# Attention by blocks of 128 query rows with the exponentials stationary, ahead of an ELU feed-forward layer, on one core

## The chip, the cores and the metric

One Trainium2 chip, one of its cores. The metric is the device time of one execution in microseconds; lower is better.

## What is computed

q, k and v are [8, 8, 576, 64] (batch, heads, sequence, head size). Each head attends with a bias that falls with the distance, within a window of 128 keys up to and including the query; the result, as 4608 tokens of 512 features, goes through two matrices with an ELU between them. Tokens are rows of batch and sequence, features are heads and head size.

```python
scores = q @ k^T / 8                       # [8, 8, 576, 576]
bias   = slope[h] * -|i - j|
scores = where((i - j >= 0) & (i - j < 128), scores + bias, -1e9)
attn   = softmax(scores)
x      = (attn @ v) as [4608, 512]
h      = x @ w_in                          # w_in [512, 2048]
g      = where(h > 0, h, exp(min(h, 0)) - 1)
out    = g @ w_out                         # w_out [2048, 512]
```

## The kernel before

All products run in f16 with f32 sums. The order of instructions on every engine is written out by hand: a list of steps, each with one round of the feed-forward layer (`hidden`, the `elu` of the round before, `output` of the block before) and, between them, the attention tasks put at that step with `at`. Engines run their own instructions in that order.

**Attention.** `load_qk` brings q and k of a batch by POOL's DMA queue with a cast to f16 (`stq`; the last 64 rows come by `load_tail`). `transposes` turns two heads on TensorE into one bank (`tp`), and VectorE copies the bank in two halves to `QK` (heads by q or k by position). Rows 64 to 127 of `QK` hold bias rows (`bias_rows`), so that the score product adds the distance bias and pushes far keys down. `scores` fills one bank (`sp`) with half of a head's windowed scores, transposed: keys are partitions, queries are columns. ScalarE takes the exponential to `E`, and `cut` on VectorE takes the minimum with `band`, which sets what is outside of the window to 0. `values` (and `values_tail` for the last 64 queries, `values_half` for batch 0) multiplies with V as the stationary operand and up to 256 exponentials as the moving one: V has 64 columns of ones beside it (`VP`), so that 64 rows of the result `av` are the value sums and the other 64 are the sum of exponentials. ScalarE makes the inverse of these as exp(-ln(s)) (`log_den`, `inv_den`), and VectorE multiplies into `xT` (`normalize`), which is features by tokens, as the hidden layer wants it. V comes by SP's queue in f32 (`load_v`, four transfers a block of 128 keys) and is cast by POOL (`cast_v`).

**Feed-forward.** `blocks` are 512 tokens each, the first one split into two of 256. `hidden` makes one bank of 128 features by 512 (or 256) tokens in four matmuls (`hp`, two banks in turn); ScalarE takes the exponential to `e`, POOL clips it to at most 1, and `elu` on VectorE takes max(e - 1, h) to `g`. `output` makes four matmuls a step (two for the narrow blocks) of the block that is 16 steps behind; after 16 of them ScalarE copies the one bank `op` to `ob`, and SP's queue writes it out. Hidden work begins at step 13, output at step 29; a batch of attention takes 16 steps.

Of the kernel before, what the change touches and what calls it, by code (L numbers as in the profile page):

```python
# [19 lines left out]
def kernel(  # L20
# [24 lines left out]
    ps_t = ctx.enter_context(tc.tile_pool(name="ps_t", bufs=1, space=PSUM))  # L45
# [3 lines left out]
    ident = const.tile([128, 128], F16, name="ident")  # L49
    band = const.tile([128, 1024], F16, name="band")  # L50
# [4 lines left out]

    QK = const.tile([128, H, 2, 768], F16, name="QK")

    VP = [const.tile([128, 5, NP, 256], F16, name=f"VP{g}", tag=f"VP{g}") for g in range(2)]
    w_in_sb = const.tile([128, 4, FF], F16, name="wi")
    w_out_sb = const.tile([128, NFC, DM], F16, name="wo")  # L60

    xT = const.tile([128, 4, RING], F16, name="xT")


    stq, stt, vf = {}, {}, {}

    def load_qk(b, w, hs=None):

        if b not in stq:
            stq[b] = stage.tile([128, 2, H, 4, D], F16, name="stq")  # L70
        h0, h1 = hs or (0, H)
# [10 lines left out]
    def load_v(b, n, behind=False):  # L82

        t = vf[b, n] = stage.tile([128, H, D], F32, name="vf", tag="vf", bufs=3)
        if behind:
            nc.gpsimd.memset(t[:, 0, 0:1], 0.0)
        if n < 4:
            for j in range(4):
                nc.sync.dma_start(
                    t[32 * j:32 * j + 32, :, :],  # L90
                    v[b, :, 128 * n + j:128 * n + 128:4, :].rearrange("h p d -> p h d"))
        else:
            nc.sync.dma_start(t[0:64, :, :], v[b, :, 512:576, :].rearrange("h p d -> p h d"))

    def cast_v(b, n):
        p = 128 if n < 4 else 64
        nc.gpsimd.tensor_scalar(  # L97
            out=VP[b % 2][0:p, n, :, :].rearrange("p a (g c) -> p (a g) c", g=2)[:, :, 0:64],
            in0=vf.pop((b, n))[0:p, :, :], scalar1=1.0, scalar2=0.0, op0=ALU.mult, op1=ALU.add)
# [12 lines left out]
    with tc.manual_schedule():  # L112

        row = const.tile([128, 1], I32, name="row")
        col = const.tile([128, 128], I32, name="col")
        posi = const.tile([128, 768], I32, name="posi")
        load_qk(0, 1, (0, 2))
        load_qk(0, 0, (0, 2))
        nc.gpsimd.iota(row, pattern=[[0, 1]], base=0, channel_multiplier=1)
        nc.gpsimd.iota(col, pattern=[[1, 128]], base=0, channel_multiplier=0)  # L120
        nc.gpsimd.iota(posi[:, 0:512].rearrange("p (n j i) -> p n j i", j=4, i=32),
                       pattern=[[128, 4], [1, 4], [4, 32]], base=0, channel_multiplier=0)
        nc.gpsimd.iota(posi[:, 512:768].rearrange("p (a b i) -> p a b i", b=2, i=64),
                       pattern=[[0, 2], [0, 2], [1, 64]], base=512, channel_multiplier=0)
# [12 lines left out]
        def small(name, n=1):
            return const.tile([128, n], F32, name=name, tag=name)
# [6 lines left out]
        kdiv, kmod, koff = (const.tile([128, 1], I32, name=n, tag=n) for n in ("kdiv", "kmod", "koff"))  # L145
        V.tensor_scalar(out=kdiv, in0=row, scalar1=5, scalar2=None, op0=ALU.logical_shift_right)
        V.tensor_scalar(out=kmod, in0=row, scalar1=31, scalar2=None, op0=ALU.bitwise_and)
        kmid = small("kmid")
        V.tensor_scalar(out=kmid, in0=kmod, scalar1=4.0, scalar2=63.5, op0=ALU.mult, op1=ALU.add)
        V.tensor_tensor(out=kmid, in0=kmid, in1=kdiv, op=ALU.add)  # L150
        rmid = small("rmid")
        V.tensor_scalar(out=rmid, in0=rowf, scalar1=63.5, scalar2=None, op0=ALU.add)

        bt = const.tile([128, 384], F32, name="bt")
        V.tensor_scalar(out=bt[:, 0:256], in0=posi[:, 0:256], scalar1=kmid, scalar2=None,
                        op0=ALU.subtract)
        V.tensor_tensor(out=bt[:, 0:256], in0=bt[:, 0:256], in1=bt[:, 0:256], op=ALU.mult)
        V.tensor_scalar(out=band[:, 0:256], in0=bt[:, 0:256], scalar1=4060.0, scalar2=BIG,
                        op0=ALU.is_le, op1=ALU.mult)
        V.tensor_copy(band[:, 256:512], band[:, 0:256])  # L160
# [3 lines left out]
        TQ = const.tile([128, 768], F16, name="TQ")  # L164
        TK = const.tile([128, 768], F16, name="TK")
        gt = const.tile([128, 768], F32, name="gt")
        g_, r_ = slice(64, 96), slice(96, 128)
        gi = const.tile([128, 768], I32, name="gi")
        V.tensor_scalar(out=gi[g_, :], in0=posi[g_, :], scalar1=gof[g_, :], scalar2=None, op0=ALU.add)
        V.tensor_scalar(out=gi[g_, :], in0=gi[g_, :], scalar1=255, scalar2=None, op0=ALU.bitwise_and)  # L170
        V.tensor_scalar(out=TQ[g_, :], in0=gi[g_, :], scalar1=134.5, scalar2=-30000.0,
                        op0=ALU.is_gt, op1=ALU.mult)
        V.tensor_scalar(out=TK[g_, :], in0=gi[g_, :], scalar1=7.5, scalar2=None, op0=ALU.is_lt)
# [4 lines left out]
        V.tensor_scalar(out=gt[r_, :], in0=posi[r_, :], scalar1=float(-MID), scalar2=None, op0=ALU.add)  # L178
        V.tensor_scalar(out=TK[r_, :], in0=gt[r_, :], scalar1=is96[r_, :], scalar2=is97[r_, :],
                        op0=ALU.mult, op1=ALU.add)  # L180
        V.tensor_scalar(out=TQ[r_, :], in0=gt[r_, :], scalar1=isx[r_, :], scalar2=is96[r_, :],  # L181
                        op0=ALU.mult, op1=ALU.add)
        for t0 in (576, 704):
            V.memset(TK[64:128, t0:t0 + 64], 0.0)
            V.memset(QK[0:64, :, 1, t0:t0 + 64], 0.0)

        def bias_rows(h):
            c = 8.0 * 2.0 ** (-8.0 * (h + 1) / H)
            nc.scalar.copy(QK[64:128, h, 0, :], TQ[64:128, :])  # L189
            V.tensor_copy(QK[g_, h, 1, :], TK[g_, :])  # L190
            V.tensor_scalar(out=QK[r_, h, 1, :], in0=TK[r_, :], scalar1=c, scalar2=None, op0=ALU.mult)  # L191

        def more_band():
            V.tensor_copy(band[:, 512:768], band[:, 0:256])
            V.tensor_copy(band[:, 768:896], band[:, 0:128])

            V.tensor_scalar(out=bt[:, 256:320], in0=posi[:, 512:576], scalar1=-384.0, scalar2=kmid,
                            op0=ALU.add, op1=ALU.subtract)
            V.tensor_scalar(out=bt[:, 320:384], in0=posi[:, 512:576], scalar1=-512.0, scalar2=rmid,
                            op0=ALU.add, op1=ALU.subtract)  # L200
            V.tensor_tensor(out=bt[:, 256:384], in0=bt[:, 256:384], in1=bt[:, 256:384], op=ALU.mult)
            V.tensor_scalar(out=band[:, 896:1024], in0=bt[:, 256:384], scalar1=4060.0, scalar2=BIG,
                            op0=ALU.is_le, op1=ALU.mult)

        def ones_v(g):
            nc.gpsimd.memset(VP[g][:, :, :, 64:128], 1.0)
            nc.gpsimd.memset(VP[g][64:128, 4, :, :], 0.0)


        ex, avt, tailt, lden, rden = {}, {}, {}, {}, {}  # L210
        HI, LO = slice(64, 128), slice(0, 64)
        NUM, DEN = (LO, HI), (HI, LO)

        def transposes(b, hp):
            t = ps_s.tile([128, 2, 2, 4, 2, 32], F16, name="tp", tag="sps")
# [7 lines left out]
            for odd in range(2):  # L223
                r = slice(64 * odd, 64 * odd + 64)
                V.tensor_copy(  # L225
                    QK[0:64, 2 * hp:2 * hp + 2, :, 0:512].rearrange(
                        "p h w (n a i) -> p (h w) n a i", a=2, i=32)[:, :, :, odd, :],
                    t[r, :, :, :, :, :].rearrange("p h w n a i -> p (h w) (n a) i"))

        def transposes_tail(b):  # L230
# [7 lines left out]
            c0 = 512 + 128 * (b % 2)  # L238
            for g in range(2):
                r = slice(64 * g, 64 * g + 64)  # L240
                V.tensor_copy(
                    QK[0:64, :, :, c0:c0 + 64].rearrange("p (n g) w c -> p n g w c", g=2)[:, :, g, :, :],
                    t[r, :, :, :])

        def scores(b, hp, g, half):

            if b == 0 and half == 0:
                s = ps_h.tile([128, 512], F32, name="sp0", tag="hp")
            else:
                s = ps_s.tile([128, 512], F32, name="sp", tag="sps")  # L250
            kq = QK[:, 2 * hp + g, :, :]
            c0 = 512 + 128 * (b % 2)
            if half == 0:
                mm = [(0, 0, 0, 256), (128, 256, 128, 256)]
            else:
                mm = [(256, 0, 256, 256), (384, 256, 384, 128), (384, 384, c0, 64), (c0, 448, c0, 64)]
            for kc, o, qc, n in mm:
                nc.tensor.matmul(s[:, o:o + n], kq[:, 1, kc:kc + 128], kq[:, 0, qc:qc + n],  # L258
                                 start=True, stop=True)
            if half == 0:  # L260
                ex[b, hp, g] = work.tile([128, 1024], F16, name="E", tag="E", bufs=9)
# [282 lines left out]
```

## Time and profile before

| | us |
|---|---|
| median of 3 runs (lowest to highest) | 396.51 (396.01 to 397.08) |
| the profiled execution | 397.05 |
| its span, from the first to the last instruction | 395.3 |

| engine | busy, us | share of the span | instructions |
|---|---|---|---|
| TensorE, matmuls (PE) | 342.1 | 87% | 2440 |
| TensorE, weight loads (PEld) | 202.6 | 51% | 2440 |
| VectorE (DVE) | 262.9 | 67% | 448 |
| ScalarE (ACT) | 246.1 | 62% | 465 |
| GpSimd (POOL) | 158.8 | 40% | 261 |

Busy time of TensorE counts each matmul from its start to its modelled end; matmuls overlap, so the busy share says where it had work, and not how close to its peak it ran. Weight loads overlap matmuls. An engine named with a q (POOLq, SPq) is the part of it that issues transfers. L361 is line 361 of the kernel.

### The profile page before, as it was taken

The numbers are of one execution on the slowest core, as the hardware profiler recorded it, in microseconds if no ns is written. First come the engines' busy times: TensorE is split into PE (matmuls) and PEld (weight loads), VectorE is DVE, ScalarE is ACT, GpSimd is POOL, SyncE is SP. The second block draws the span as 40 slices with busy tenths as digits, with TensorE's granted clock in tenths as the row PEclk, the third lists the DMA queues.
The fourth block names the chain that finished last, engine by engine and source line by source line (L and its number), as shares of the span: only waits on it lengthen the run. The fifth ranks groups of instructions, "written<-read, shape, count | busy, mean of one in ns | idle before, by whom it ended". The sixth has DMA issues, their size and how long they took to land.

```text
span 395.3 us, 6838 instructions
## 1 busy us (share of the span) xinstructions
PE 342.1 (87%) x2440; PEld 202.6 (51%) x2440; DVE 262.9 (67%) x448; ACT 246.1 (62%) x465; POOL 158.8 (40%) x261
## 2 busy tenths in 40 slices
PE   1234775998999899999999999999999999999984
PEld 0112553675565455567765555555666544444431
DVE  6776677688788877777776778777876533343300
ACT  1445565788777866877687778776777643443411
POOL 8692173264365246334623452433222333333300
PEclk9999998799999999999999999999999999999999
DMA  6999999149339138632933293311111112121122
GB/s 85 158 163 188 192 172 149 24 62 157 80 39 169 39 89 106 104 77 64 146 82 82 46 142 80 90 44 41 29 27 28 28 28 53 27 55 27 37 72 54
DMA packets 75267, 32.97 MB, mean 83 GB/s; under 512 B 50144, under 2 KB 70624, under 8 KB 75232
## 3 DMA queue, kind: packets, MB, share of 16 engines
q0 software_dynamic: 29408, 13.63, 27.8%
q1 hardware_dynamic: 45824, 18.89, 22.0%
q8 instruction: 19, 0.31, 0.3%
q14 instruction: 16, 0.13, 0.1%
HBM read 36.70 MB, written 9.44 MB: 117 GB/s over the span
## 4 chain that ended last, share of the span: by engine, by line
PE 70%; DVE 18%; ACT 4%; issue 3%; POOL 2%; POOLq 0%; ACTq 0%; DVEq 0%
PE hp L361 28%; PE op L399 27%; PE sp L258 6%; PE av L277 5%; DVE QK L225 4%; DVE g L372 3%; PE tp L219 3%; DVE xT L331 2%; DVE xT L345 2%; DVE E L266 1%; DVE QK L190 1%; DVE QK L191 1%; PE avh L288 1%; DVE xT L302 1%; ACT ldent L337 1%
## 5 line engine op out<-in xcount | busy, mean ns | idle before, releaser
L365 POOL TENSOR_SCALAR e<-e 128x512 f32<-128x512 f32 (+1 forms) x160 | 93.5, 585 | 206.6 <-ACT e L364 205.9
L361 PE MATMUL hp<-xT,wi 128*128 128x512 f16 (+5 forms) x768 | 153.4, 330 | 11.5 <-DVE g L372 10.8
L372 DVE SCALAR_TENSOR_TENSOR g<-e,hp 128x512 f16<-128x512 f32 (+1 forms) x160 | 101.0, 634 | 78.0 <-POOL e L365 75.5
L399 PE MATMUL op<-wo,g 128*128 128x512 f16 x576 | 148.5, 379 | 2.9 <-ACT ob L403 2.9
L364 ACT ACTIVATE e<-hp 128x512 f32<-128x512 f32 (+1 forms) x160 | 88.8, 555 | 94.3 <-PE hp L361 92.0
L361 PEld LDWEIGHTS <-wi 128*128 128x128 f16 x768 | 73.0, 99 | 79.1 <-issue 17.9
L262 ACT ACTIVATE E<-sp 128x512 f16<-128x512 f32 x128 | 72.9, 595 | 11.7 <-PE sp L258 11.0
L399 PEld LDWEIGHTS <-g 128*128 128x128 f16 x576 | 51.2, 98 | 46.1 <-issue 4.0
L258 PE MATMUL sp<-QK 128*128 128x256 f16 (+2 forms) x384 | 47.9, 249 | 21.8 <-DVE QK L191 21.5
L225 DVE COPY QK<-tp 64x1024 f16<-64x1024 f16 x64 | 43.9, 687 | 13.2 <-PE tp L219 12.0
L258 PEld LDWEIGHTS <-QK 128*128 128x128 f16 x384 | 34.0, 102 | 35.8 <-DVE QK L191 24.8
L266 DVE TENSOR_TENSOR E<-E,band 128x1024 f16<-128x1024 f16 (+1 forms) x72 | 45.4, 636 | 1.9 <-ACT E L262 1.6
L331 DVE TENSOR_TENSOR xT<-av,rden 64x512 f16<-64x512 f32 x56 | 38.5, 688 | 1.7
L320 ACT ACTIVATE lden<-av 64x512 f32<-64x512 f32 x56 | 32.9, 587 | 2.1 <-PE av L277 1.5
L403 ACT COPY ob<-op 128x512 f32<-128x512 f32 x36 | 21.5, 597 | 17.9 <-PE op L399 17.9
L277 PE MATMUL av<-E,VP 128*128 128x256 f16 x224 | 31.4, 264 | 0.5
L277 PEld LDWEIGHTS <-VP 128*128 128x128 f16 x224 | 22.0, 100 | 11.2 <-issue 1.2
L219 PE MATMUL tp<-ident,stq 128*128 128x128 f16 x256 | 21.5, 231 | 6.6 <-DMA stq<-in_k_dram 4.6
L97 POOL TENSOR_SCALAR VP<-vf 128x512 f16<-128x512 f32 (+1 forms) x40 | 25.1, 629 | 4.3 <-DMA vf<-in_v_dram 4.3
L219 PEld LDWEIGHTS <-stq 128*128 128x128 f16 x256 | 16.6, 104 | 7.4 <-DMA stq<-in_k_dram 4.6
L324 ACT ACTIVATE rden<-lden 128x512 f32<-128x512 f32 x28 | 17.6, 629 | 0.9
L189 ACT COPY QK<-TQ 64x768 f16<-64x768 f16 x8 | 6.2, 825 | 10.7 <-DVE TQ L181 10.6
(65 smaller groups left out, 149.4 us busy)
## 6 DMA issues: line engine op xcount, KB each, us to landing
vf<-in_v_dram SPq DMA_DIRECT2D x128, 64.0 KB, 2.5
out_dram<-ob SPq DMA_DIRECT2D x128, 64.0 KB, 1.7
stq<-in_k_dram POOLq DMA_DIRECT2D x7, 512.0 KB, 6.5
stq<-in_q_dram POOLq DMA_DIRECT2D x7, 512.0 KB, 8.0
wi<-in_moe_w_in_dram POOLq DMA_DIRECT2D x4, 512.0 KB, 8.7
wo<-in_moe_w_out_dram POOLq DMA_DIRECT2D x4, 512.0 KB, 21.2
vf<-in_v_dram SPq DMA_DIRECT2D x8, 128.0 KB, 2.9
out_dram<-ob SPq DMA_DIRECT2D x8, 128.0 KB, 2.3
```

The lines of the kernel that those rows point to most:

```text
L219: nc.tensor.transpose(t[:, g, w, :, j, :], stq[b][:, w, 2 * hp + g, 2 * j:2 * j + 2, :].rearrange("p a d -> p (a d)"), ident)
L225: V.tensor_copy(QK[0:64, 2 * hp:2 * hp + 2, :, 0:512].rearrange("p h w (n a i) -> p (h w) n a i", a=2, i=32)[:, :, :, odd, :], t[r, :, :, ...
L258: nc.tensor.matmul(s[:, o:o + n], kq[:, 1, kc:kc + 128], kq[:, 0, qc:qc + n], start=True, stop=True)
L262: nc.scalar.activation(ex[b, hp, g][:, 512 * half:512 * half + 512], s, AF.Exp, scale=0.125)
L266: V.tensor_tensor(out=e, in0=e, in1=band[:, c0:c1], op=ALU.min)
L277: nc.tensor.matmul(a[:, o:o + w], VP[b % 2][:, n, hp, lo:lo + 128], ex[b, hp, g][:, e:e + w], start=(i == 0), stop=(i == 3))
L331: V.tensor_tensor(out=xT[NUM[g], hp, c:c + 512], in0=avt.pop((b, hp, g))[NUM[g], :], in1=rden[b, hp][DEN[g], :], op=ALU.mult)
L361: nc.tensor.matmul(p[:, u0:u1], w_in_sb[:, c, fc * 128:(fc + 1) * 128], xT[:, c, x0:x0 + u1 - u0], start=(c == 0), stop=(c == 3))
L364: nc.scalar.activation(e[:, 0:n], p[:, 0:n], AF.Exp)
L365: nc.gpsimd.tensor_scalar(out=e[:, 0:n], in0=e[:, 0:n], scalar1=1.0, scalar2=0.0, op0=ALU.min, op1=ALU.max)
L372: V.scalar_tensor_tensor(out=gs[t][:, fc, 0:n], in0=es.pop((t, fc))[:, 0:n], scalar=1.0, in1=hps.pop((t, fc))[:, 0:n], op0=ALU.subtract, o ...
L399: nc.tensor.matmul(ops[t], gs[t][:, fc, ts * 128:(ts + 1) * 128], w_out_sb[:, fc, :], start=(fc == 0), stop=(fc == NFC - 1))
```

## The change

Scores are made for blocks of 128 queries: one step of the schedule fills one bank (`scores(b, s)`), with four heads of the first block, two heads of a middle block (two key blocks each), or four heads of the last 64 queries. The exponentials of a bank (`EX`, four tiles in turn) become the stationary operand of the value product, 128 queries at a time, and V with one column of ones the moving one (65 columns), so that the result has queries as partitions, and the sum of exponentials is one number for each query and head. VectorE takes its reciprocal and multiplies with it (`normalize`); the logarithms go. Since x now has tokens as partitions, `turn` transposes it on TensorE (four transposes for 128 tokens, a bank `xps`) and copies it to `xT`, on ScalarE for batch 0 and on VectorE for the others.

`QK` has two copies, one each for even and odd batches. The bias rows are filled for four or three heads at once in the first; POOL copies them to the second (`second_qk`, 16 copies in steps 4 to 14). Of the two copies of a transposed bank ScalarE makes one (for batch 1 both). V of batches 0 and 1 comes by POOL's queue with the cast (`load_v4`, rows of 1 KB) and is put in place by VectorE (`place_v4`, four copies a block); the other batches as before.

Every hidden bank is 512 wide: in the first two blocks of tokens it holds four feature groups of 128 tokens, in the next four two groups of 256, then one of 512. There are 9 blocks for 10, hidden work begins at step 7 (`LAG`), output at step 23. In the last block the output takes turns with a bank of `ps_h`.

The core of the diff (what the functions above replace is left out):

```diff
...
+    QK = [one([128, H, 2, 640], F16, f"QK{i}") for i in range(2)]
+    VP = [one([128, 5, H, VW], F16, f"VP{i}") for i in range(2)]
+    EX = [one([128, 576], F16, f"EX{i}") for i in range(4)]
...
+    def load_v4(b):
+
+        vs[b] = stage.tile([128, H, 4, D], F16, name="vs", tag="vs", bufs=2)
+        nc.gpsimd.dma_start(vs[b].rearrange("p h j d -> p h (j d)"),
+                            v[b, :, 0:512, :].rearrange("h (p j) d -> p h (j d)", j=4))
+
+    def load_v4_tail(b):
+        nc.gpsimd.dma_start(VP[b % 2][0:64, 4, :, 0:D],
+                            v[b, :, 512:576, :].rearrange("h s d -> s h d"))
+
+    def place_v4(b, n):
+        for j in range(4):
+            V.tensor_copy(VP[b % 2][32 * j:32 * j + 32, n, :, 0:D],
+                          vs[b][32 * n:32 * n + 32, :, j, :])
...
+        load_qk(0, 1, 0, 2)
+        load_qk(0, 0, 0, 2)
+        nc.gpsimd.iota(col, pattern=[[1, 128]], base=0, channel_multiplier=0)
+        for h0, h1 in ((2, 4), (4, 8)):
+            load_qk(0, 1, h0, h1)
+            load_qk(0, 0, h0, h1)
+        load_v4(0)
+        for i in range(4):
+            load_wi(i)
...
+        def second_qk(h, w):
+            nc.gpsimd.tensor_scalar(
+                out=QK[1][64:128, h, w, 0:576], in0=QK[0][64:128, h, w, 0:576],
+                scalar1=1.0, scalar2=0.0, op0=ALU.mult, op1=ALU.add)
...
+        BANKS = [(0, 0), (0, 1)] + [(i, p) for i in (1, 2, 3) for p in range(4)] + [(4, 0), (4, 1)]
...
+                if odd or b == 1:
+                    nc.scalar.copy(o, i)
+                else:
+                    V.tensor_copy(o, i)
...
+        def scores(b, s):
+            i, p = BANKS[s]
+            t = ps_s.tile([128, 512], F32, name="sp", tag="sps")
+            qk = QK[b % 2]
+
+            def mm(o, h, kc, qc, n):
+                nc.tensor.matmul(t[:, o:o + n], qk[:, h, 1, kc:kc + 128], qk[:, h, 0, qc:qc + n],
+                                 start=True, stop=True)
+
+            if i == 0:
+                for l in range(4):
+                    mm(128 * l, 4 * p + l, 0, 0, 128)
+            elif i < 4:
+                for l in range(2):
+                    mm(256 * l, 2 * p + l, 128 * i - 128, 128 * i, 128)
+                    mm(256 * l + 128, 2 * p + l, 128 * i, 128 * i, 128)
+            else:
+                for l in range(4):
+                    mm(128 * l, 4 * p + l, 384, 512, 64)
+                    mm(128 * l + 64, 4 * p + l, 512, 512, 64)
+            e = ex[b, s] = EX[count[0] % 4]
+            count[0] += 1
+            nc.scalar.activation(e[:, 0:512], t, AF.Exp, scale=0.125)
+
+        def cut(b, s):
+            i = BANKS[s][0]
+            e = ex[b, s][:, 0:512]
+            V.tensor_tensor(out=e, in0=e, in1=band[0 if i == 0 else 1 if i < 4 else 2], op=ALU.min)
...
+                avt[b, i, half] = ps_v.tile([128, 4, D + 1], F32, name="av", tag="av")
...
+            def mm(l, c, n, h, st, sp):
+                nc.tensor.matmul(a[:, l, :], e[:, c:c + 128], vp[:, n, h, 0:D + 1], start=st, stop=sp)
...
+            r = work.tile([128, 4], F32, name="rden", tag="rden", bufs=2)
+            V.reciprocal(out=r, in_=a[:, :, D])
+            V.tensor_tensor(out=xnt[b, i][:, 4 * half:4 * half + 4, :], in0=a[:, :, 0:D],
+                            in1=r.unsqueeze(2).broadcast_to([128, 4, D]), op=ALU.mult)
+
+        def turn(b, i):
+            n = 128 if i < 4 else 64
+            t = ps_x.tile([128, 4, 128], F16, name="xps", tag="xps")
+            x = xnt.pop((b, i)).rearrange("p (c h) d -> p c (h d)", h=2)
+            for c in range(4):
+                nc.tensor.transpose(t[:, c, :], x[:, c, :], ident)
+            o = (b * S + 128 * i) % RING
+            (nc.scalar.copy if b == 0 else V.tensor_copy)(xT[:, :, o:o + n], t[:, :, 0:n])
...
+        width = lambda t: 128 if t < 2 else 256 if t < 6 else 512
...
+        def hidden(t, j):
+            w, c0, f0, nf = place(t, j)
+            p = hps[t, j] = ps_h.tile([128, 512], F32, name="hp", tag="hp")
+            a = (512 * t + c0) % RING
+            cuts = [(0, w, a)] if a + w <= RING else [(0, RING - a, a), (RING - a, w, 0)]
+            for l in range(nf):
+                fc = f0 + l
+                for u0, u1, x0 in cuts:
+                    for c in range(4):
+                        nc.tensor.matmul(
+                            p[:, l * w + u0:l * w + u1], w_in_sb[:, c, fc * 128:(fc + 1) * 128],
+                            xT[:, c, x0:x0 + u1 - u0], start=(c == 0), stop=(c == 3))
...
+                if last and ts % 2:
+                    ops[t] = ps_h.tile([128, DM], F32, name="op2", tag="hp")
...
+        LAG = 7
...
+        at(1, place_v4, 0, 0)
+        at(1, band_others)
         for w in (1, 0):
...
+            at(1, load_tail, 0, w)
+        at(1, load_v4_tail, 0)
+        for w in (1, 0):
+            at(1, load_qk, 1, w)
+            at(1, load_tail, 1, w)
+        for n in (1, 2, 3):
+            at(2 * n, place_v4, 0, n)
...
         for i in range(4):
...
+            at(3 + i, load_wo, i)
+            pass
+        for h in range(H):
+            for w in range(2):
+                at(4 + h + 3 * w, second_qk, h, w)
+        at(7, load_v4, 1)
+        at(7, load_v4_tail, 1)
+        for n in range(4):
+            at(13 + n, place_v4, 1, n)
+
+        for b in range(B):
+            s0 = 16 * b
+            for s in range(16):
+                i, p = BANKS[s]
+                at(s0 + s + (b == 0 and s == 1) * 0, scores, b, s)
+                at(s0 + s + 1, cut, b, s)
+                at(s0 + s + 2, values, b, s)
+                half = p if i in (0, 4) else p // 2
+                if i in (0, 4) or p % 2:
+                    at(s0 + s + 3, normalize, b, i, half)
+                    if half:
+                        at(s0 + s + 4, turn, b, i)
+            if b + 1 < B:
+                for hp in range(NP):
+                    at(s0 + (5 + 3 * hp if b else 9 + 2 * hp), transposes, b + 1, hp)
+                at(s0 + 15, transposes_tail, b + 1)
+            if b + 2 < B:
+                for n in range(5):
+                    at(s0 + 18 + 2 * n, load_v, b + 2, n)
+                    at(s0 + 21 + 2 * n, cast_v, b + 2, n)
                 for i, w in enumerate((1, 0)):
...
+                    at(s0 + 16 + 2 * i, load_qk, b + 2, w)
+                    at(s0 + 17 + 2 * i, load_tail, b + 2, w)
...
```

## Rows read from the trace of the kernel before

**Rows 1.** The page: busy time of the engines, and TensorE's busy tenths.

```profile
PE 342.1 (87%) x2440; PEld 202.6 (51%) x2440; DVE 262.9 (67%) x448; ACT 246.1 (62%) x465; POOL 158.8 (40%) x261
...
PE   1234775998999899999999999999999999999984
```

**Rows 2.** The chain of waits in order of time: start us, us, what.

```profile
243.27 1.02 PE hp L361 x4
...
280.47 1.02 PE hp L361 x4
...
382.64 3.63 PE op L399 x16
...
386.98 3.63 PE op L399 x16
```

**Rows 3.** Busy time (instructions) in stretches: PE, PEld, DVE, ACT, POOL, clock, DMA.

```profile
45.00:73.70 28.70, 20.55 (x184) 16.03 (x182) 19.01 (x41) 18.60 (x46) 14.27 (x26) 0.88 0.95 142
...
243.27:280.47 37.20, 37.08 (x264) 21.19 (x264) 28.51 (x44) 27.56 (x52) 12.72 (x22) 1.00 0.22 50
```

**Rows 4.** TensorE's instructions in order of time, 246 to 247 us: start us, us.

```profile
246.68 0.10 PEld L315 LDWEIGHTS <-VP 128*128 128x128 f16 x1
...
246.71 0.10 PEld L314 LDWEIGHTS <-VP 128*128 128x128 f16 x1
...
246.80 0.61 PE L219 MATMUL tp<-ident,stq 128*128 128x128 f16 x8
```

**Rows 5.** Instructions in order of time near the start; and those that read `wo`.

```profile
22.22 0.76 DVE L266 TENSOR_TENSOR E<-E,band 128x512 f16<-128x512 f16 x2
...
45.08 1.04 PE L361 MATMUL hp<-xT,wi 128*128 128x256 f16 x4
...
L399 PE MATMUL op<-wo,g x576: 376/379/390, 73.7 to 390.2; 128*128 128x512 f16 x192
```

**Rows 6.** Groups by line and shape: busy us, mean ns, idle before.

```profile
L372 DVE SCALAR_TENSOR_TENSOR g<-e,hp 128x512 f16<-128x512 f32 x128 | 87.9, 688 | 71.5 <-POOL e L365 69.4
L225 DVE COPY QK<-tp 64x1024 f16<-64x1024 f16 x64 | 43.9, 687 | 13.2 <-PE tp L219 12.0
...
L266 DVE TENSOR_TENSOR E<-E,band 128x512 f16<-128x512 f16 x16 | 6.9, 459 | 0.2
L302 DVE TENSOR_TENSOR xT<-avh,rdenh 64x256 f16<-64x256 f32 x16 | 6.8, 422 | 7.6 <-ACT rdenh L297 7.4
...
L158 DVE TENSOR_SCALAR band<-bt 128x256 f16<-128x256 f32 x1 | 0.3, 293 | 0.0
...
L202 DVE TENSOR_SCALAR band<-bt 128x128 f16<-128x128 f32 x1 | 0.2, 228 | 0.0
```

**Rows 7.** POOL's transfers in order of time, 21 to 34 us.

```profile
21.23 2.29 POOL L103 DMA_DIRECT2D wi<-in_moe_w_in_dram  x3
23.49 0.91 POOL L72 DMA_DIRECT2D stq<-in_k_dram  x1
24.36 0.91 POOL L72 DMA_DIRECT2D stq<-in_q_dram  x1
...
33.09 0.74 POOL L106 DMA_DIRECT2D wo<-in_moe_w_out_dram  x1 [2.20 <-DMA wi<-in_moe_w_in_dram]
```

**Rows 8.** Issue to landing, 12 to 60 us: `wi`, `stq`, `wo`.

```profile
DMA to landing us min/median/max: 5.7/7.8/10.0
...
DMA to landing us min/median/max: 13.9/15.5/17.0
...
DMA to landing us min/median/max: 18.2/21.2/22.4
```

**Rows 9.** The clip of the hidden bank of 243.27 us.

```profile
245.01 0.61 POOL L365 TENSOR_SCALAR e<-e 128x512 f32<-128x512 f32 x1 [1.73 <-ACT e L364]
```

**Rows 10.** Issue to landing of `stq`: 180 to 215 us, and 100 to 140.

```profile
DMA to landing us min/median/max: 5.9/6.0/6.0
...
DMA to landing us min/median/max: 8.3/8.9/9.6
```

More of the change, by code (lines that the diff above doesn't have):

```diff
@@ L160 @@
[L160 removed]
+        g_, r_ = slice(64, 96), slice(96, 128)
         gof = small("gof")
         V.tensor_scalar(out=gof, in0=rowf, scalar1=-8.0, scalar2=1024.0, op0=ALU.mult, op1=ALU.add)
[L164 to L169, printed above, removed]
+        TQ = one([128, 576], F16, "TQ")
@@ L241, in transposes_tail @@
                 V.tensor_copy(
-                    QK[0:64, :, :, c0:c0 + 64].rearrange("p (n g) w c -> p n g w c", g=2)[:, :, g, :, :],
+                    QK[b % 2][0:64, :, :, 512:576].rearrange("p (n g) w c -> p n g w c", g=2)[:, :, g, :, :],
                     t[r, :, :, :])
-        def scores(b, hp, g, half):
-            if b == 0 and half == 0:
-                s = ps_h.tile([128, 512], F32, name="sp0", tag="hp")
-            else:
-                s = ps_s.tile([128, 512], F32, name="sp", tag="sps")
-            kq = QK[:, 2 * hp + g, :, :]
-            c0 = 512 + 128 * (b % 2)
-            if half == 0:
[L254 to L261, printed above, removed]
-            nc.scalar.activation(ex[b, hp, g][:, 512 * half:512 * half + 512], s, AF.Exp, scale=0.125)
@@ L280, in values_half @@
-        def values_half(hp, half):
-            a = avt[0, hp, half] = ps_v.tile([128, 512], F32, name="avh", tag="av")
-            parts = (FIRST, SECOND)[half]
-            for g in range(2):
-                lo = 64 * g
-                for i, (n, o, e, w) in enumerate(parts):
-                    o += 256 * (g - half)
-                    nc.tensor.matmul(a[:, o:o + w], VP[0][:, n, hp, lo:lo + 128],
-                                     ex[0, hp, g][:, e:e + w], start=(i == 0), stop=(i == len(parts) - 1))
@@ L306, in values_tail @@
-        def values_tail(b, hp):
-            if b not in tailt:
-                tailt[b] = ps_t.tile([128, 2, NP, 64], F32, name="avtail")
-            vp = VP[b % 2]
-            for g in range(2):
-                e = ex.pop((b, hp, g))
-                o = tailt[b][:, g, hp, :]
-                lo = 64 * g
-                nc.tensor.matmul(o, vp[:, 3, hp, lo:lo + 128], e[:, 896:960], start=True, stop=False)
-                nc.tensor.matmul(o, vp[:, 4, hp, lo:lo + 128], e[:, 960:1024], start=False, stop=True)
@@ L350 @@
-        blocks = [(0, 256), (256, 256)] + [(512 * i, 512) for i in range(1, NTOK // 512)]
-        hps, es, gs, ops = {}, {}, {}, {}
-        def hidden(t, fc):
-            c0, n = blocks[t]
-            p = hps[t, fc] = ps_h.tile([128, 512], F32, name="hp", tag="hp")
-            a = xcol(c0)
-            cuts = [(0, n)] if a + n <= RING else [(0, RING - a), (RING - a, n)]
-            for u0, u1 in cuts:
-                x0 = xcol(c0 + u0)
-                for c in range(4):
-                    nc.tensor.matmul(p[:, u0:u1], w_in_sb[:, c, fc * 128:(fc + 1) * 128],
-                                     xT[:, c, x0:x0 + u1 - u0], start=(c == 0), stop=(c == 3))
-            e = es[t, fc] = work.tile([128, 512], F32, name="e", tag="e")
-            nc.scalar.activation(e[:, 0:n], p[:, 0:n], AF.Exp)
-            nc.gpsimd.tensor_scalar(out=e[:, 0:n], in0=e[:, 0:n], scalar1=1.0, scalar2=0.0,
-                                    op0=ALU.min, op1=ALU.max)
@@ L389, in rows_of, with output @@
             return r
-        def output(t, i):
-            c0, n = blocks[t]
-            nts = n // 128
-            for idx in range(i * nts, (i + 1) * nts):
-                ts, fc = divmod(idx, NFC)
-                if fc == 0:
+        def output(t, j):
+            ts, f0 = j // 4, 4 * (j % 4)
+            last = t == NTB - 1
+            if f0 == 0:
+                if last and ts % 2:
+                    ops[t] = ps_h.tile([128, DM], F32, name="op2", tag="hp")
+                else:
                     ops[t] = ps_o.tile([128, DM], F32, name="op", tag="op")
+            for fc in range(f0, f0 + 4):
                 nc.tensor.matmul(ops[t], gs[t][:, fc, ts * 128:(ts + 1) * 128], w_out_sb[:, fc, :],
                                  start=(fc == 0), stop=(fc == NFC - 1))
-                if fc == NFC - 1:
-                    ob = work.tile([128, DM], F32, name="ob", tag="ob")
-                    nc.scalar.copy(ob, ops[t])
-                    for p0, rows in rows_of(c0 + 128 * ts):
-                        nc.sync.dma_start(rows, ob[p0:p0 + rows.shape[0], :])
+            if f0 == 12:
+                ob = work.tile([128, DM], F32, name="ob", tag="ob")
+                nc.scalar.copy(ob, ops[t])
+                for p0, rows in rows_of(512 * t + 128 * ts):
+                    nc.sync.dma_start(rows, ob[p0:p0 + rows.shape[0], :])
         tasks = {}
@@ L492 @@
-        for b in range(1, B):
-            p = base(b - 1) if b > 1 else F
-            for n in range(5):
-                at(p + 2 + 2 * n, load_v, b, n)
-                at(p + 6 + 2 * n, cast_v, b, n)
-            if b >= 2:
-                p = base(b - 1)
+        LAG = 7
+        transposes(0, 0)
+        fill_q(0)
+        fill_k()
+        for h in range(4):
+            k_term(h)
+        transposes(0, 1)
+        transposes(0, 2)
+        band_first()
+        at(0, fill_q, 4)
+        for h in range(4, H):
+            at(0, k_term, h)
```

359 lines of the change are left out of this document (137 added, 222 removed).

## The prediction

> **What bounds the kernel now.** I read the page first, then the stretches, the chain of waits, the engines' order of time, and the POOL queue's landings. TensorE is busy 87% of the span and short of work only in the first eight or nine slices [rows 1]. One batch of the middle is the stretch from the chain's hidden-layer product at 243.27 us to the one at 280.47 us, 16 steps of the schedule later [rows 2]: 37.20 us, TensorE busy 37.08, VectorE 28.5, ScalarE 27.6 [rows 3]. I count its columns: hidden layer 32768, output 32768, scores 8192, values 8192, transposes 4608, together 86528; at 2.4 GHz 36.05 us, with 264 matmuls at 2.5 ns each 36.7. (2.5 ns is what eight 128-column transposes leave over: (0.61 - 0.219)/7 = 56 ns apart against 53.3 of streaming; 0.219 is the length of one, the pace is the row's [rows 4].) So the middle is at TensorE's limit, with 0.5 us a batch to spare. The last 16 steps lose 0.7 us at each of three changes of the one output bank (4.33 between groups that stream 3.63), and 4.7 us lie between the end of the last group and the span's end [rows 2]. All else is lost at the start: the first hidden matmul is at 45.08 us, the first output matmul at 73.7 [rows 5], and between them TensorE is busy 20.55 of 28.70 us [rows 3].
>
> **The steady state after the change.** TensorE's columns per batch: hidden and output as before, scores 8192 as before (72 matmuls for 48), values 72 x 65 = 4680 for 8192, turning x 2560 more: 85576, or 35.7 us. Matmuls rise from some 260 to 330-460, so 0.3 us more at 2.5 ns. About nothing is gained or lost. That holds if a short matmul with its own 128-column weight load keeps its pace. The trace has this: in the tail product of 64 columns the weight loads start 0.03 us apart, although each lasts 0.10 [rows 4]; so 65 columns cost 30 ns and I take that. The Trainium skill speaks against it (TensorE: Matmul & The Clock Gate, Back-to-back issue gap): in a stream of load-and-matmul pairs it gives about 81 ns at 128 columns. By that the short matmuls still to run after step 23 (some 1500) would cost an estimated 40 us or more; these rows, at 56 and 30 ns, do not agree.
>
> VectorE per batch: 16 ELUs at 0.69, 16 cuts of 512 at 0.46 (before: 8 of 1024), ten normalizations (product 0.42 as L302, a reciprocal of four numbers, not in the trace, 0.05 to 0.3, taken 0.2), five turns (512 elements from a bank, half of L225) at 0.42, four transpose copies at 0.69, 0.8 of tail: 30.2 us [rows 6]. Of 37 that is hidden. Before it was 28.5. ScalarE gives up all logarithms and inverse exponentials and takes four copies of some 1 us (1024 elements; bounds 0.69, VectorE's time for them, and 1.4): clearly below its 27.6. Both lie beside TensorE.
>
> **The start.** The order on the POOL queue decides it. Before, V went by the SP queue; now V of batches 0 and 1 goes by POOL with the cast, and all transfers there land in order. Per 512 KB: w_in landed between 21.2+5.7 = 26.9 and 22.8+10.0 = 32.8, two chunks, 2.95 us each; k and q of batch 1 at 37.4 and 41.4, 4.0 to 4.6 beside V's loads; w_out from 46.1 to 55.5, 3.1 each [rows 7, 8]. Also the queue takes no ninth transfer: the fourth w_out load is the 22nd and waited for the 14th, the last w_in [rows 7].
> New order: q, k of batch 0 (till some 11 us, two chunks at issue pace), V 3.5 (14.5), w_in 4 x 2.9 (26), three tails 2.2 (28.3; an eighth of a chunk each, 0.37 by bytes, twice that taken), k and q of batch 1 at 4.0 (36.3), two tails (37.8), w_out 4 x 3.0 (49.8), V of batch 1 3.7: **53.5 us**. At 2.95 for every chunk it is 48; at the shared 4.3 for the cast rows of q, k, v and 3.1 for the rest, 57.
> The steps: VectorE, busy with tables, bias rows and copies, made the first cut at 22.2 us [rows 5]; its new list of the like is about as long, and I take 21. Steps 2 to 6 hold it some 1.6 us each (a cut, half a normalization, half a placing, below), so step 7, the first hidden bank, comes near 29 (45.08 before). But this early start is not kept. Step 9 transposes batch 1, TensorE in order behind q, which lands at 36.3; and POOL, whose V loads of step 7 are the 23rd and 24th and wait for the 15th and 16th, is held as long, with the clip of step 8 behind it. So step 10 is near 39. Step 13 is near 48 (POOL has two copies of bias rows a step, taken at 0.65, near the clip's 0.61 [rows 9], bounds 0.5 and 0.9, and the clip: 1.9 to 2 a step; three steps from step 10, and elu and products behind the last). There VectorE stands at the first placing of V of batch 1, with cut and ELU behind it, and TensorE two steps later: it waits to 53.5.
> A placing is four copies of 512 f32 to f16 on 32 rows. L158 and L202 give 0.065 us for 128 more elements, so 0.42 each [rows 6]; bounds 0.3 (two-thirds overlapped) and 0.7; taken 0.43, 1.7 a step. Rest of step 13: 2.5. Steps 14 to 16: ELU 0.69, placing 1.7, cut 0.46, normalization 0.4: 3.3 each, 9.9. Steps 17 to 22: TensorE needs 1.45 a step, the ring of two hidden banks 1.55, the middle's step is 2.33; I take 1.9, 11.4. That is 77.3. q of batch 2 is issued in step 18, near 70, lands 5.9 to 9.6 later [rows 10] (I take 6.7, since little else is under way) and is wanted near 74.5: 2.2 more. **Step 23, the first output, at 79.5 us** (bounds 73 and 87), later than the 73.7 of before.
>
> **What is left then.** Columns: hidden 8 of 9 blocks 262144, output 294912, scores 53760, values 31460, turns 17408, transposes 26624: 686308, 286.0 us; 2992 matmuls at 2.5 ns, 7.5. Sum 293.4. Before, at its 73.7, some 711500 columns were left, 301.4 us with overhead, and it took 316.9 to the last matmul. The 15 us between are where it loses: the second of the 256-column blocks is still to run, each step with a full round of hidden, exponential, clip and ELU for half the work. That is the loss that the narrow banks (always 512 columns, of several feature groups) take away.
> To it: 0.5 us a batch as now, eight times, 4.0; the end 4.7; the gaps between the last groups are gone, since the output takes turns with a free bank. One thing is new: q of batch b+2 is issued only three steps ahead (18 before). The clip ahead of it on POOL ends 2.35 us into the step (245.01 + 0.61 - 243.27) [rows 2, 9], the landing takes 5.9 to 9.6 [rows 10], so q is there 8.3 to 12 us after step 18 starts; TensorE wants it three steps of 2.3 later, behind 0.86 of hidden and some 0.55 of turn, values and scores: at 8.3. Late by 0 to 3.6, five times; taken 0.6, nearer the quiet end: 3.0.
> **Sum: 79.5 + 293.4 + 4.0 + 4.7 + 3.0 = 384.6 us** of span, against 395.3; with the 1.75 around it 386.4, against 397.05; to the median, 0.54 less: **386 us**.
>
> **Rivals.**
> *The loads come sooner.* If chunks land at 2.95 us without V beside them, V of batch 1 is there when step 13 is (48), step 23 is at 73, and q is never late: 386 - 6.5 - 3 = 376. For it: the SP queue is empty at the start. Against: q and k have shorter rows than w_in, and landed slower.
> *q late each batch* (ends on the other side). TensorE stands in order at the first transpose of each batch. At the row with 9.6 us this is 3.6 five times: 386 + 15 = 401; from 2.7 us a batch the change is no gain. For it: V's loads of the same batch now start in the same steps. Against: landings of 5.9 in the quiet middle.
> *Weight loads come out.* If the stationary exponentials load without overlap, at the 100 ns of a load [rows 4] for 30, 484 value products cost 34 us more: 420. It decides from 53 ns on. Against it: the tail's loads 30 ns apart. The page of the Trainium skill named above would set such a pace.
> *The change doesn't do what it says.* If VectorE, 30.2 of 37, falls behind (heavy steps have ELU, turn, normalization, cut and copy, 2.6 us and more), the batch takes 38.2, the early gain is eaten: 394 to 397.
>
> **Chances.** The forecast 0.50 (its own range 380 to 392), loads sooner 0.21, q late 0.13, weight loads 0.06, VectorE behind 0.10. Below 0.3% (1.2 us, about what a measurement here can tell) is no change. Faster: the first two and half of the last, and a part of q late: 0.78. Same 0.06, slower 0.16. Range 372 to 397: it takes in both bounds of step 23 and q late up to the break-even.
>
> **What the profile will show.** First hidden matmul near 29 us, then a hole before 37 to 40 (TensorE on q of batch 1, POOL on a landing) and a second one, VectorE on V of batch 1, ending near 53; first output near 79; value products some 30 ns apart; batches of 37 us with VectorE at 30; last four output groups without gaps. Wrong would be: first output before 70 (loads faster) or after 88; TensorE idle on the stq load in every batch; batches above 38 us.

## The result, and the profile after

Over the runs of the first comparison the changed kernel takes 384.81 us (median of 4, 382.51 to 385.44) against 396.26 for the kernel before; the ratio is 0.9701, 95% interval 0.9656 to 0.9747. Where the runs of a kernel fall into two groups, the times and ratios here and below are those of the faster group. Forecast were 386 us and faster. The total came out nearly right, but two terms of the sum were off, in opposite directions: the first output came 4.3 us sooner than forecast, and late loads of q cost more, 11.4 us (first experiment) for the 5.2 of the sum.

The page of the changed kernel, busy time and the slices that answer to [rows 1]:

```profile
PE 340.9 (89%) x3552; PEld 239.0 (62%) x3552; DVE 252.6 (66%) x602; ACT 214.8 (56%) x354; POOL 158.5 (41%) x249
...
PE   2337768699979999999999999999999999999995
```

TensorE has 1112 more matmuls and the same busy time. It is near full from the ninth slice on, with a dent in the 12th slice. ScalarE has lost 31 us of work, VectorE 10.

Its chain of waits in order of time, to be read against [rows 2, 5]:

```profile
63.72 7.22 DMA stq<-in_q_dram
...
102.21 7.92 DMA stq<-in_q_dram
...
143.10 6.75 DMA stq<-in_q_dram
...
181.32 6.54 DMA stq<-in_q_dram
...
219.18 6.64 DMA stq<-in_q_dram
```

The first hidden matmul is at 29.7 us (45.08 before), the first output at 75.2 (73.7 before). In the second line 75.2 and 377.9 are the first and the last start of an output matmul:

```profile
29.68 1.91 PE L383 MATMUL hp<-xT,wi 128*128 128x128 f16 x16
...
L424 PE MATMUL op<-wo,g x576: 376/379/634, 75.2 to 377.9; 128*128 128x512 f16 x192
...
364.28 13.97 PE L424 MATMUL op<-wo,g 128*128 128x512 f16 x64 [0.72 <-ACT ob L428]
```

The third line holds the last four output groups, which ran without a gap between them, as forecast. The transfer that brings q is on the chain in each of these batches: it runs from POOL's issue through the whole transfer to the transposes. How long TensorE itself stood, in its own order of time (the bracket is the idle time ahead of the instruction, and what ended it):

```profile
70.98 0.82 PE L263 MATMUL tp<-ident,stq 128*128 128x128 f16 x6 [2.98 <-DMA stq<-in_q_dram]
...
110.17 0.51 PE L263 MATMUL tp<-ident,stq 128*128 128x128 f16 x6 [2.03 <-DMA stq<-in_q_dram]
...
149.89 0.51 PE L263 MATMUL tp<-ident,stq 128*128 128x128 f16 x6 [0.91 <-DMA stq<-in_q_dram]
...
225.87 0.51 PE L263 MATMUL tp<-ident,stq 128*128 128x128 f16 x6 [0.81 <-DMA stq<-in_q_dram]
```

Six transposes, not eight, stand behind the wait: the first two of a bank are of k, which was there. The five waits from 110 to 264 us are 5.2 us together.

The start on POOL, with landings, to be read against [rows 7, 8]: the issues of q and V of batch 1, and the landing of each:

```profile
20.31 0.91 POOL L76 DMA_DIRECT2D stq<-in_q_dram  x1 [1.79 <-DMA wi<-in_moe_w_in_dram]
...
34.55 0.94 POOL L89 DMA_DIRECT2D vs<-in_v_dram  x1
...
DMA to landing us min/median/max: 12.0/12.0/12.0
...
DMA to landing us min/median/max: 11.3/11.3/11.3
```

q landed at 20.31 + 12.0 = 32.3 us, V at 34.55 + 11.3 = 45.9. VectorE came to the placing of V right then, and did not wait:

```profile
47.02 0.69 DVE L395 SCALAR_TENSOR_TENSOR g<-e,hp 128x512 f16<-128x512 f32 x1 [0.51 <-POOL e L388]
47.63 2.01 DVE L98 COPY VP<-vs 32x512 f16<-32x512 f16 x4
...
50.72 1.96 DVE L98 COPY VP<-vs 32x512 f16<-32x512 f16 x4
...
54.32 1.17 DVE L98 COPY VP<-vs 32x512 f16<-32x512 f16 x4
...
57.60 1.65 DVE L98 COPY VP<-vs 32x512 f16<-32x512 f16 x4
```

Busy time in a batch of the middle (the columns of [rows 3]):

```profile
219.18:257.14 37.96, 37.15 (x399) 27.86 (x397) 26.65 (x63) 23.97 (x40) 16.21 (x27) 1.00 0.55 91
```

37.96 us for 16 steps against 37.20; the 0.8 more is the wait for q (with q in time, in the first experiment, the same 16 steps take 37.2). VectorE is busy 26.65 us (28.5 before), ScalarE 23.97 (27.6 before).

### The profile page after: what moved, and what is told of

It reads as the page before. It is cut to its first block, busy times and chain, and to the rows that moved or that the text cites. A ratio compares the mean times of both kernels' runs of the same rounds, so it can differ in the third digit from the quotient of the medians.

```text
span 383.0 us, 9037 instructions
## 1 busy us (share of the span) xinstructions
PE 340.9 (89%) x3552; PEld 239.0 (62%) x3552; DVE 252.6 (66%) x602; ACT 214.8 (56%) x354; POOL 158.5 (41%) x249
## 4 chain that ended last, share of the span: by engine, by line
PE 68%; DMA 12%; DVE 11%; ACT 2%; POOL 2%; issue 1%; SPq 1%; ACTq 0%; POOLq 0%; DVEq 0%
PE hp L383 27%; PE op L424 27%; DMA stq<-in_q_dram 11%; PE sp L297 6%; PE av L331 4%; PE tp L263 3%; DVE VP L98 2%; POOL e L388 2%; DMA out_dram<-ob 1%; PE xps L360 1%; ACT e L387 1%; DVE EX L318 1%; DVE g L395 1%; ACT ob L428 1%; POOL QK L245 1%
## 5 line engine op out<-in xcount | busy, mean ns | idle before, releaser
L388 POOL TENSOR_SCALAR e<-e 128x512 f32<-128x512 f32 x144 | 91.5, 635 | 190.1 <-ACT e L387 188.8
L383 PE MATMUL hp<-xT,wi 128*128 128x128 f16 (+5 forms) x1344 | 153.0, 262 | 1.7 <-DVE g L395 1.5
L395 DVE SCALAR_TENSOR_TENSOR g<-e,hp 128x512 f16<-128x512 f32 x144 | 98.4, 683 | 76.5 <-POOL e L388 75.4
L387 ACT ACTIVATE e<-hp 128x512 f32<-128x512 f32 x144 | 86.1, 598 | 100.3 <-PE hp L383 93.7
L383 PEld LDWEIGHTS <-wi 128*128 128x128 f16 x1344 | 109.7, 100 | 48.4 <-issue 2.6
L313 ACT ACTIVATE EX<-sp 128x512 f16<-128x512 f32 x128 | 76.1, 595 | 8.5 <-PE sp L297 7.5
L297 PE MATMUL sp<-QK 128*128 128x128 f16 (+1 forms) x576 | 52.7, 220 | 5.6 <-ACT QK L273 3.9
L318 DVE TENSOR_TENSOR EX<-EX,band 128x512 f16<-128x512 f16 x128 | 56.9, 446 | 0.1
L273 ACT COPY QK<-tp 64x1024 f16<-64x1024 f16 x36 | 36.2, 1009 | 33.6 <-DVE QK L275 32.6
L331 PE MATMUL av<-VP,EX 128*128 128x65 f16 x576 | 39.7, 196 | 7.3 <-DVE EX L318 7.2
L263 PE MATMUL tp<-ident,stq 128*128 128x128 f16 x256 | 23.5, 235 | 18.9 <-DMA stq<-in_q_dram 11.4
```

Source lines behind the costliest of these rows:

```text
L263: nc.tensor.transpose(t[:, g, w, :, j, :], stq[b][:, w, 2 * hp + g, 2 * j:2 * j + 2, :].rearrange("p a d -> p (a d)"), ident)
L273: nc.scalar.copy(o, i)
L297: nc.tensor.matmul(t[:, o:o + n], qk[:, h, 1, kc:kc + 128], qk[:, h, 0, qc:qc + n], start=True, stop=True)
L313: nc.scalar.activation(e[:, 0:512], t, AF.Exp, scale=0.125)
L318: V.tensor_tensor(out=e, in0=e, in1=band[0 if i == 0 else 1 if i < 4 else 2], op=ALU.min)
L331: nc.tensor.matmul(a[:, l, :], e[:, c:c + 128], vp[:, n, h, 0:D + 1], start=st, stop=sp)
```

## The experiments

All times are medians, beside runs of the kernel before on the same chip (395.3 to 395.9 us); ratios are to those.

**q and k issued eight steps sooner.**

```diff
-                    at(s0 + 16 + 2 * i, load_qk, b + 2, w)
+                    at(s0 + 8 + 2 * i, load_qk, b + 2, w)
```

> k and q of batch b+2 are issued eight steps sooner (8 and 10 steps after the batch's start for 16 and 18). Theory: TensorE stands in order at the transposes of each batch for a late q: 3.0 us in batch 2, 2.0 in batch 3 with some 2 us of half clock behind it, 0.7 to 0.9 in the four others, about 10 us. Then 375 to 377 us, with no wait of TensorE on q in any batch from 2 on. Rival: the other engines are behind at the same place, and the wait only hides that; then 382 to 385.

373.39 us, ratio 0.9452 (0.9427 to 0.9477): 11.4 us below the changed kernel, and 1.6 below the range of the theory. Two waits of TensorE by cause (total, times, longest) and the instructions that read `wo` (the first and last start of an output matmul):

```profile
PE hp L383 <- DVE g L395: 3.7, 6, 1.9
PE tp L263 <- DMA stq<-in_q_dram: 3.4, 3, 1.9
```

```profile
L424 PE MATMUL op<-wo,g x576: 376/379/381, 70.4 to 365.8; 128*128 128x512 f16 x192
```

The three waits on q that are left are those of the first 13 us, none in a later batch. The first output is at 70.4, and from there to the last output matmul 295.4 us; 293.4 was the forecast for TensorE's columns and matmuls alone. So little but TensorE's work is left behind the first output (2 us), and the late loads alone had given back half of what the change can bring. The rival falls.

**V of batch 1 by SP and POOL's cast.**

```diff
-        at(7, load_v4, 1)
-        at(7, load_v4_tail, 1)
-        for n in range(4):
-            at(13 + n, place_v4, 1, n)
+        for n, (sl, sc) in enumerate(((8, 13), (9, 14), (10, 15), (14, 17), (16, 19))):
+            at(sl, load_v, 1, n)
+            at(sc, cast_v, 1, n)
```

> V of batch 1 by the SP queue and POOL's cast as in the kernel before; the 16 copies that place it on VectorE in steps 13 to 16 are gone, 0.6 MB leaves the POOL queue. Theory: from about 47 us on, the landing of V holds nothing (it lands as VectorE comes to it) but the placing, 1.2 to 2.0 us a step, is on the path; step 23 comes some 5 us sooner: 379 to 381 us. Rival: ScalarE's copies of batch 1's transposes (2.0 us every other step) and POOL set the same pace; then 384 to 385.

383.21 us, ratio 0.9701 (0.9677 to 0.9724): 1.6 less than the changed kernel, too little to tell the two sides apart. The first output is at 74.9 (75.2), and TensorE's wait for q of batch 2 grew:

```profile
70.68 0.82 PE L263 MATMUL tp<-ident,stq 128*128 128x128 f16 x6 [3.71 <-DMA stq<-in_q_dram]
```

Some 0.7 us of what VectorE saved came back as waiting. With both edits the question is cleaner:

> Both edits of before together: q and k eight steps sooner, V of batch 1 by SP and POOL's cast. With the late q alone put right the time was 373.4; with V alone 383.2, and there TensorE then waited 3.7 us for q of batch 2. Theory: what VectorE's placing costs came back as a wait for q, so now it shows: 368 to 371 us. Rival: POOL and ScalarE set the pace of steps 13 to 16 all the same: 373 to 374.

371.65 us, ratio 0.9395 (0.9359 to 0.9431), 1.7 below the run with q alone and 0.65 above what the theory gave. First output 68.2 against 70.4. So taking out the four placings, 6.8 us of VectorE, was worth some 2 us: most of them lay beside other work. Part or all of the 2 us is clock: with the placings TensorE waits 1.33 and 1.94 us for VectorE's cut near 50 and 53 us, and from 55 to 60 us its granted clock is 0.53; without them neither wait is there, and it is 1.00. In the stretch of the placings the run without them (q not in time there; columns of [rows 3]) has ScalarE busy 13.95 of 15 us, and VectorE 9.89 (10.69 and 13.93 in the changed kernel):

```profile
45.00:60.00 15.00, 12.81 (x222) 11.75 (x220) 9.89 (x23) 13.95 (x22) 11.76 (x19) 0.96 0.13 28
```

The run with q alone, behind the placings:

```profile
55.00:60.00 5.00, 5.00 (x58) 4.71 (x56) 4.74 (x14) 3.33 (x5) 0.76 (x1) 0.53 0.00 2
```

The two edits together are the best version of the study.

**The price of a short matmul.**

```diff
-                nc.tensor.matmul(a[:, l, :], e[:, c:c + 128], vp[:, n, h, 0:D + 1], start=st, stop=sp)
+                for twice in range(2):
+                    nc.tensor.matmul(a[:, l, :], e[:, c:c + 128], vp[:, n, h, 0:D + 1],
+                                     start=st and twice == 0, stop=sp and twice == 1)
```

> Each value product is issued twice into the same sum (numerator and denominator double, the quotient stays). 576 more matmuls of 65 columns, 484 of them after the first output. Theory: TensorE is the bound from there on and a short matmul with its own weight load costs 30 ns: 14 to 17 us more, 398 to 402. Rival A: each weight load costs its 100 ns: 48 to 57 more, 433 to 442. Rival B: TensorE is not the bound in the middle: under 388.

395.5 us (median of 7 runs, 392.2 to 397.5), ratio 0.9997 (0.9960 to 1.0034): 10.7 us more than the changed kernel, 2.5 under the range of the theory and far from both rivals. The runs spread over 5 us, too much for a price. With q in time it shows:

> q and k sooner, and each value product issued twice into the same sum (the quotient stays). Without late loads the price of 576 short matmuls shows by itself: 27 to 30 ns each for the 484 behind the first output and no more for the others: 386 to 388 us. Rival: a part of them is hidden in gaps, 377 to 384; or weight loads come out, over 395.

388.19 us, ratio 0.9810 (0.9775 to 0.9844): 14.8 us more than without the second product, which is 31 ns for each of the 484 behind the first output, just above the theory (388, 30 ns). The trace counts a weight load for each added product too (4128 loads for 3552). The trace of the changed kernel has the same pace: four value products in 0.28 us, of which one lasts 0.192, start 29 ns apart; 16 hidden products of 128 columns in 1.06 us, one 0.219, are 56 ns apart.

```profile
106.41 1.06 PE L383 MATMUL hp<-xT,wi 128*128 128x128 f16 x16
107.30 0.39 PE L360 MATMUL xps<-ident,xn 128*128 128x128 f16 x4
107.53 0.28 PE L331 MATMUL av<-VP,EX 128*128 128x65 f16 x4
```

So a weight load of 0.1 us beside each of them adds nothing that shows, and what lengthens TensorE's list lengthens the kernel.

**Half-filled banks.** Blocks and hidden layer of the kernel before put into the changed one:

```diff
-        width = lambda t: 128 if t < 2 else 256 if t < 6 else 512
+        blocks = [(0, 256), (256, 256)] + [(512 * i, 512) for i in range(1, NTB)]
...
-        LAG = 7
+        LAG = 11
```

> The first 512 tokens again as two blocks of 256 in half-filled hidden banks (16 steps each, as in the kernel before), hidden from step 11, all else as after the change. Theory: each step is a full round of hidden, exponential, clip and ELU whatever its width, so 16 more steps of about 1.8 us for no more work: first output of a full block near 110 us, 393 to 398 us in all, no better than the kernel before. Rival: the gain comes from the sooner start of the hidden layer and from the lighter attention; then 384 to 388.

404.26 us, ratio 1.0234 (1.0210 to 1.0258): slower than the kernel before, and by more than the theory said. TensorE waited here longer for q, from 60 us on:

```profile
PE tp L263 <- DMA stq<-in_q_dram: 15.2, 6, 3.7
```

The first two of the six waits, 3.75 and 3.01 us, lie among half-filled rounds, whose hidden products start 1.4 to 1.6 us apart, so three steps cover less of a transfer. Two later ones, 3.65 and 2.88, stand behind landings of 8.2 and 8.7 us, for 6.5 to 7.9 in the changed kernel; why these took longer is open. The pair with q in time separates the two causes:

> Half-filled hidden banks for the first 512 tokens (hidden from step 11), now with q and k sooner, so that late loads don't blur it. Theory: 16 more rounds at 1.8 us with 1024 columns less in each of 32: against full banks with the same first step (the other run of this pair) 10 to 14 us more, 386 to 392 us. Rival: late loads made the excess of the earlier run with half banks; then within 5 us of the other run.

> q and k sooner, full narrow banks, but hidden work begins at step 11 (7 before). Theory: the steps before the first output are paced by VectorE, ScalarE and POOL, so four more steps before it cost 1.5 to 1.9 us each, less what attention then has done ahead (four steps of 0.5 us on TensorE): 377 to 380 us. Rival: the loads set the start, and hidden work only fills their gaps: 373 to 375.

Half-filled banks 385.23 us, ratio 0.9740 (0.9700 to 0.9781); full banks from the same step 376.87, ratio 0.9520 (0.9481 to 0.9559). The difference, 8.4 us, is what the full banks bring, somewhat less than the 10 to 14 expected, and net of 576 more matmuls that the narrow blocks need; the rest of the 404.26 (19 us) was late loads. Four steps later cost 3.5 us, 0.9 a step, at the lower edge; the rival of that run, that the loads set the start, doesn't hold, or it would have cost nothing.

**Full banks alone, in the kernel before.** The first 512 tokens as one block there; hidden begins at step 27, since there the tokens of a batch are ready only when all of its heads are done.

```diff
-        blocks = [(0, 256), (256, 256)] + [(512 * i, 512) for i in range(1, NTOK // 512)]
+        blocks = [(512 * i, 512) for i in range(NTOK // 512)]
...
+            if t == 0:
+                for l in range(2):
+                    f, x0 = 2 * (fc % 8) + l, 256 * (fc // 8)
...
-        LAG = F + 5
+        LAG = F + 19
```

> The kernel before with one part of the change: the first 512 tokens as one block of 512-column hidden banks (two feature groups of 256 tokens), 9 blocks for 10. Its attention has the tokens of a batch ready only when all heads are done, so hidden begins at step 27 (13 before). Theory: the half-filled rounds are the loss, but the later start gives most of it back: 389 to 395. Rival A: full banks alone are the gain, 381 to 386. Rival B: the late start costs more than they bring, 397 to 404.

400.76 us, ratio 1.0117 (1.0071 to 1.0163): rival B. The first hidden product is at 63.14 us and the first output at 99.2, 25 us later than in the kernel before. With the old order of heads full banks do not pay; the blocks of 128 query rows deliver the tokens in order.

**VectorE's slack.** From batch 2 on both copies of a transposed bank on VectorE, with q in time:

```diff
-                if odd or b == 1:
+                if b < 2 and (odd or b == 1):
```

> q and k sooner; and from batch 2 on VectorE makes both copies of a transposed bank (ScalarE gives its one up): 2.7 us more of VectorE in a batch. Theory: VectorE has some 9 us a batch to spare beside TensorE, nothing changes: 372.5 to 374.5. Rival: its longest steps hold TensorE; then 1 to 2.7 us a batch, 379 to 390.

373.72 us, ratio 0.9447 (0.9416 to 0.9478): the same as with q alone, 373.39. A stretch of the middle, 37.86 us long, has VectorE busy 31.09 us (27.43 with q alone), and TensorE all of it:

```profile
181.32:219.18 37.86, 37.86 (x404) 28.38 (x402) 31.09 (x69) 20.91 (x39) 16.96 (x26) 1.00 0.55 92
```

## Why the prediction was right, step by step

| step | forecast | measured |
|---|---|---|
| first hidden matmul | 29 us | 29.7 |
| q of batch 1 landed | 36.3 | 32.3 |
| VectorE at the first placing of V | 48 | 47.6 |
| V of batch 1 landed | 53.5 | 45.9 |
| placing, a step | 1.7 | 1.2 to 2.0 |
| wait for q of batch 2 | 2.2 | 3.0 |
| first output | 79.5 | 75.2 |
| first output to the last matmul | 300.4 | 303.1 |
| of it, waits for q | 3.0 | 5.2 |
| end | 4.7 | 4.7 |
| span | 384.6 | 383.0 |

**The middle.** Right: TensorE stays the bound at the same length of batch, apart from q; short matmuls keep their 30 and 56 ns, by the trace and by doubling them; VectorE and ScalarE lie beside it. The pace that the Trainium skill gives (TensorE: Matmul & The Clock Gate, Back-to-back issue gap) for a stream of load-and-matmul pairs does not appear here. VectorE's 30.2 us a batch was 26.65; one reason is that its instructions overlap (one that starts at 221.52 us and lasts 0.67 has the next at 222.11), which adding up single durations misses.

**The start.** The step that failed is the pace of POOL's queue, and with it both holes that were to hang on landings. I took 4.0 us for 512 KB of q, k and 3.7 for V, from rows in which V's own loads shared the engines, and 13.5 for the w_out loads with two tails. From the last of the three tails (27.3 us) k and q took 5.0 us for 8, w_out and the tails 10.6, and V 3.0. So q landed 4 and V 7.6 us sooner, the latter even below the 48 that I gave as the lower bound. That the sharing made the difference is likely, but no run shows it by itself. The first hole, TensorE on q of batch 1 and POOL on a landing, did not open: q was there at 32.3, the transposes of step 9 came after it and waited for a score exponential, and POOL had its waits on landings before 27 us, none at V's loads at 34.55.

```profile
38.40 0.61 PE L263 MATMUL tp<-ident,stq 128*128 128x128 f16 x8 [0.69 <-ACT EX L313]
```

Nor did the second, VectorE on V. That step 13 still came within half a microsecond of the forecast is no proof of its reasons. From 29.88 to 47.6 us VectorE waits for nothing but POOL's clip (total, times, longest), and POOL's groups in that stretch (busy, mean ns, idle ahead) hold no wait on a landing:

```profile
DVE g L395 <- POOL e L388: 4.8, 5, 1.4
```

```profile
L245 POOL TENSOR_SCALAR QK<-QK 64x576 f16<-64x576 f16 x12 | 8.2, 681 | 1.0
L388 POOL TENSOR_SCALAR e<-e 128x512 f32<-128x512 f32 x6 | 3.9, 653 | 2.5 <-ACT e L387 2.2
```

Twelve copies of bias rows and six clips are 12.1 us for the six steps, 2.0 each, as the forecast had them; three DMA issues of 2.4 us and waits of 2.2 us on ScalarE's exponential fill most of the rest of the 17.7. The forecast had the same end from a hole of 10 us and three steps behind it. So the start went as the rival "loads come sooner" had it, except that steps 13 to 23 took 27.6 us for its 25, with 3.0 for q of batch 2 among them.

**Late q.** Forecast as a term of 0.6 us a batch, with 3.6 as its bound; the trace has 2.0, 0.9, 0.7, 0.8 and 0.8. Its place and cause are as said: issue behind the clip of step 18, landing 6.5 to 7.9 us later, three steps too few. The forecast's own formula (2.35 us to the issue, q wanted at 8.3) gives 0.6 to 2.0 with these landings; its form held, and the landing, 7.9 us for the first of the five, was taken too short. TensorE idle on this load in every batch was named as a sign of being wrong: it came, beside a forecast that had itself a wait in every batch. What the sum left out is what follows a wait. Behind the 2.03 us at 108 to 110 us the granted clock of the stretch falls, and the same 16 products take 1.80 us for 1.06:

```profile
105.00:120.00 15.00, 12.97 (x138) 9.77 (x136) 8.07 (x20) 7.41 (x13) 4.48 (x8) 0.89 0.61 104
```

```profile
111.38 1.80 PE L383 MATMUL hp<-xT,wi 128*128 128x128 f16 x16
```

0.89 of 15 us is 1.65 us lost. The same stands behind the first wait, of 2.98 us:

```profile
71.60 1.91 PE L383 MATMUL hp<-xT,wi 128*128 128x128 f16 x16
...
70.00:75.00 5.00, 4.02 (x51) 4.02 (x52) 2.15 (x6) 2.11 (x3) 1.27 (x3) 0.66 0.46 70
```

0.66 of 5 us is up to 1.7 us more. With the load in time the kernel gains 11.4 us, and 3.0 and 5.2 of waits, 1.65 and 1.7 of clock are 11.5. The first output came 4.8 us sooner, for a wait of 3.0 and this clock. So the term was 5.2 in the sum (2.2 and 3.0) and 11.4 on the chip. The start without it was 70.4 us for a forecast 77.3. The two errors gave a total only 1 us off: the agreement of the totals is partly luck.

**Where the gain comes from.** Measured with q in time: full banks 8.4 us, four steps' sooner start of the hidden layer 3.5; full banks without the new attention -5. The other 10 us between the kernel before and the run with half-filled banks and q in time (395.3 to 385.2) belong to the rest of the change; no run splits them. The forecast had named the half-filled rounds as the place of the loss (15 us between the columns and the time taken); that place is right, and the size includes what the old order of heads forced.

## What to carry to other kernels

When a schedule is counted in steps, the lead of a load must be counted in microseconds: three steps of 2.3 us were less than clip, issue and landing together, and the engine that works in order pays each time. Where one engine is at its limit in the middle, add up its columns from the first moment at which it is full to the end; that sum was right here to 1% with q in time (293.4 us for 295.4), and what remains to be gained lies ahead of that moment and in its waits. Price a queue by rows in which nothing shares it, if the change takes the sharer away.

## What was not expected of the hardware

A wait of TensorE of 2.03 us in a full stretch was followed by products at half the pace (16 products of 128 columns in 1.80 us for 1.06), and the granted clock of the 15 us around it was 0.89; so was the wait of 2.98 us (1.91 us; 0.66 from 70 to 75 us). Waits of 0.7 to 0.9 us in the later batches left the granted clock of their stretches at 1.00. But in the first run with half-filled banks a wait of 2.88 us was followed by products at full pace, with the granted clock at 1.00 on both sides of it. So the length of a wait alone did not decide here:

```profile
210.58 0.51 PE L263 MATMUL tp<-ident,stq 128*128 128x128 f16 x6 [2.88 <-DMA stq<-in_q_dram]
...
205.00:210.00 5.00, 2.70 (x32) 1.90 (x28) 2.17 (x5) 2.22 (x4) 1.96 (x3) 1.00 1.38 220
210.00:215.00 5.00, 4.42 (x45) 3.18 (x46) 2.88 (x7) 2.68 (x4) 0.61 (x1) 1.00 0.20 41
```
